# Gate and up projections wholly in 64-row tiles, q, k and v projections as single pieces, in a scheduled attention-and-MLP kernel

## The chip, the core and the metric

The kernel runs on one core of one Trainium2 chip. The metric is the device time of one execution in microseconds (us). The kernel before took 230.38 us (median of 3 runs, 229.4 to 230.75).

## What is computed

The input is x, 2048 rows of 448 in bf16. With xn = layernorm(x), two blocks work on xn, and the output is x + A(xn) * silu(B(xn)).

```
q, k, v = xn @ wq, xn @ wk, xn @ wv          # 448 -> 16 heads of 28, four segments of 512 rows
per segment: p = softmax(q k^T * scale + causal mask);  a_dot = p v
             a_mem = (phi(q) M) / (phi(q) z + 1e-6)   # memory of the segments before
             o = g * a_mem + (1 - g) * a_dot;  M += phi(k)^T v;  z += sum phi(k)
A(xn) = o @ wo
B(xn) = (gelu(xn @ w_gate) * (xn @ w_up)) @ w_down    # 448 -> 1792 -> 448
```

## The kernel before, in words

**Stages.** The four segments of 512 rows go through stages in the order G0, A0, A1, G1, A2, G2, A3, G3, D3 (table `ORDER`). G is the gate and up projection of a segment with its gelu. A is the attention of a segment. Into the A stages the kernel fits the down projection of the segment before (`down`, L1155), the output projection (`finish`, L1185), the memory's read and update (L898, L860) and the q, k and v projections of segments to come (`Unit.product`, L714). D3 is the down and output projection of the last segment.

**The order of work.** Every piece of work is an `Op` with a name, its engines with assumed durations, what it depends on, and the buffers it takes. `arrange` (L276) lists all ops in one order: at each step it takes the piece that can start first, or, among those within 0.2 us, the one with the lowest priority. The priorities come from the table `PRIO` (about 1000 numbers), and `STEP` says behind which of the ten score steps of an attention stage a filler piece is let go. The result is a fixed instruction order on each engine, which every engine then works through from front to back, waiting on semaphores. The planner also knows the array's mode (`Op.mode`): "full" for 128 contraction rows, "r64" for two tiles of 64 rows side by side, "r32" for four of 32 rows (the scores, where a head has 28 channels), "c32" for four column tiles (p times v).

**Buffers.** PSUM's eight banks are one pool `B_`: four in two pairs (`pp`), four single (`ps`). A chunk of gate and up takes two banks, a score step two pairs, any other product one bank. SBUF has, among others, five slots `pt` for the softmax numerators of a score step.

**Contraction over 448.** 448 is three times 128 and a rest of 64. In `gate_up` each of the 14 chunks of 128 hidden columns needs gate and up, each over 448 rows. `full` (L1089) makes the six matmuls over 128 rows (three for gate, then three for up, 512 columns each). The rests of gate and up lie in the two halves of one weight tile `wh_sb`, so `halves` (L1104) makes both rests at once, as two 64-row tiles side by side. To change modes seldom, the rests of four chunks are made in one visit: the visit ends two chunks and begins the next two (`VISITS`), four visits per segment. `hidden` then runs gelu on ScalarE (L1114) and the product of gelu and up on VectorE (L1119) into hT.

**Projections.** A q, k or v unit is one block of 128 rows by 448 columns: three matmuls over 128 rows (`Unit.full`), and a rest over 64 rows. Two units with even and odd block make their rests in one `visit` side by side (L714 again). In `project` the two full parts and the visit are three pieces, which the planner may set apart.

**Attention.** A score step has four matmuls side by side into two bank pairs, one or two times (L985), then two exponentials of 1024 columns on ScalarE (L1000), then causal masks on POOL (L1011). p times v is L1047, its copy out of PSUM L883. The exponentials need another table in ScalarE than gelu, so each passage between G and A stages has an ACT_TABLE_LOAD.

**Start.** Segment 0 is turned by TensorE (`turned_by_pe`, L596): once centred for the projections, once normalised (xn) for gate and up, four blocks each. The copies out of PSUM are L598, on VectorE or ScalarE. Meanwhile ScalarE also evicts projections (L752), squares weights for a bound that is checked once (L1248), and makes the first phi(k) (L826). The other segments' xn is turned by DMA (L685). Weights and x come by DMAs from the SP and ACT queues (L490).

## Time and profile before

| | |
|---|---|
| median of 3 runs | 230.38 us (229.4 to 230.75) |
| span of the profiled execution, first to last instruction | 227.6 us |
| TensorE (PE) busy | 217.5 us (96%), 1557 matmuls recorded |
| VectorE (DVE) busy | 152.7 us (67%) |
| ScalarE (ACT) busy | 152.7 us (67%) |
| GpSimd (POOL) busy | 129.3 us (57%) |
| granted TensorE clock | 0.999 |

The profile tells of one execution by its span, the time from its first to its last instruction. The times of runs are device times of whole executions, so they hold some 2.8 us outside the span (230.38 less 227.6). In rows of groups, the columns are line, engine and operation with "out<-in" by the program's names, shapes and count, then busy us and mean ns of one, then idle time of the engine just before them and what ended it. In rows of the timeline they are start, length, engine, line and operation, with idle time before and its releaser in brackets. A matmul's mean ns holds the way through the array, so start to start is the pace, not the mean. "PEld" is TensorE's weight load, which runs beside matmuls.

### The profile page before, as it was taken

How to read it: one execution, taken by the hardware profiler on the slowest of the kernel's cores; microseconds unless marked ns; L12 is line 12 of the kernel's file. 1: busy time of each engine (PE TensorE's matmuls, PEld its weight loads, DVE VectorE, ACT ScalarE, POOL GpSimd, SP SyncE). 2: the span in 40 equal slices, each digit the busy share in tenths (PEclk: the TensorE clock that was granted, in tenths of full speed). 3: DMA queues.
4: the chain of work that ended last, by engine and by line, in shares of the span. 5: the costliest groups of instructions: out<-in, count | busy, mean ns of one | idle time of the engine just before them, and what ended most of it. 6: DMA issues, size and time to landing. Idle time of an engine off the chain costs nothing.

```text
span 227.6 us, 4462 instructions
## 1 busy us (share of the span) xinstructions
PE 217.5 (96%) x1557; PEld 95.6 (42%) x1570; DVE 152.7 (67%) x287; ACT 152.7 (67%) x212; POOL 129.3 (57%) x221
## 2 busy tenths in 40 slices
PE   7999999889999999999999999999999999999991
PEld 2544433333544434344444444344444434444561
DVE  3799998767965795674875587863746463647262
ACT  4799645999898779432788898443878875346120
POOL 8601400579588599603599989853199477604500
PEclk9999999999999999999999999999999999999999
DMA  6999569964434763217603132272500018135011
GB/s 215 222 357 259 103 152 248 237 128 83 48 72 72 183 127 74 76 38 201 186 20 68 27 71 69 59 196 59 140 1 4 12 45 225 31 84 125 4 40 50
DMA packets 44708, 25.11 MB, mean 110 GB/s; under 512 B 30808, under 2 KB 40856, under 8 KB 44680
## 3 DMA queue, kind: packets, MB, share of 16 engines
q1 hardware_dynamic: 43704, 24.05, 44.7%
q10 hardware_dynamic: 976, 0.71, 1.0%
q8 instruction: 14, 0.23, 0.4%
q14 instruction: 14, 0.11, 0.2%
HBM read 16.00 MB, written 2.98 MB: 83 GB/s over the span
## 4 chain that ended last, share of the span: by engine, by line
PE 82%; ACT 10%; DVE 2%; issue 2%; ACTq 1%; POOL 1%; DVEq 0%; POOLq 0%
PE ps L1155 16%; PE ps L1089 15%; PE pp L1089 14%; PE ps L714 11%; PE pp L985 5%; PE ps L1185 5%; PE ps L1047 4%; ACT pt L1000 3%; PE ps L1104 3%; PE pp L1104 3%; PE pp L1155 2%; ACT pt L1248 2%; PE ps L898 1%; PE ps L860 1%; PE ps L1221 1%
## 5 line engine op out<-in xcount | busy, mean ns | idle before, releaser
L1000 ACT ACTIVATE pt<-pp 128x1024 bf16<-128x1024 f32 x75 | 73.3, 1037 | 11.8 <-PE pp L985 9.9
L1011 POOL TENSOR_SCALAR_AFFINE_SELECT pt<-pt 128x256 bf16<-128x256 bf16 x128 | 54.3, 448 | 26.0 <-ACT pt L1000 23.6
L1155 PE MATMUL ps<-wd_sb,hT 128*128 128x448 bf16 x182 | 39.0, 354 | 0.4 <-DVE qs L750 0.4
L1114 ACT ACTIVATE gl<-pp 128x512 bf16<-128x512 f32 x28 | 15.8, 595 | 29.0 <-PE pp L1104 23.2
L1155 PEld LDWEIGHTS <-hT 128*128 128x128 bf16 x210 | 18.8, 98 | 20.1 <-issue 5.0
L1119 DVE TENSOR_TENSOR hT<-gl,pp 128x512 bf16<-128x512 bf16 x28 | 18.4, 682 | 11.6 <-ACT gl L1114 11.5
L1119 DVE TENSOR_TENSOR hT<-gl,ps 128x512 bf16<-128x512 bf16 x28 | 18.7, 677 | 11.0 <-ACT gl L1114 8.4
L1114 ACT ACTIVATE gl<-ps 128x512 bf16<-128x512 f32 x28 | 16.6, 597 | 13.0 <-PE ps L1089 6.1
L1089 PEld LDWEIGHTS <-wu_sb 128*128 128x128 bf16 x168 | 16.4, 98 | 20.1 <-issue 0.3
L1089 PEld LDWEIGHTS <-wg_sb 128*128 128x128 bf16 x168 | 14.9, 98 | 22.5 <-issue 7.1
L909 POOL TENSOR_TENSOR om<-om,rb 128x512 f32<-128x512 f32 x12 | 14.9, 1268 | 15.9 <-DMA rb<-rdr 15.8
L714 PEld LDWEIGHTS <-xnT 128*128 128x128 bf16 (+1 forms) x192 | 15.0, 96 | 20.6 <-issue 10.1
L1089 PE MATMUL pp<-xnT,wu_sb 128*128 128x512 bf16 x84 | 22.7, 379 | 0.3
L1089 PE MATMUL ps<-xnT,wu_sb 128*128 128x512 bf16 x83 | 22.5, 379 | 0.2
L956 POOL TENSOR_TENSOR oT<-oa,om 128x512 bf16<-128x512 f32 x12 | 16.0, 1337 | 11.5 <-DVE oa L953 11.5
L1089 PE MATMUL ps<-xnT,wg_sb 128*128 128x512 bf16 x81 | 22.1, 380 | 0.3 <-issue 0.3
L1089 PE MATMUL pp<-xnT,wg_sb 128*128 128x512 bf16 x76 | 21.2, 380 | 0.4 <-issue 0.3
L831 POOL TENSOR_SCALAR e<-e 128x896 bf16<-128x896 bf16 (+1 forms) x12 | 12.8, 1070 | 10.9 <-ACT e L826 10.9
L985 PE MATMUL pp<-qT,kT 32*128 32x512 bf16 (+3 forms) x238 | 17.0, 301 | 2.0 <-ACT pt L1000 1.8
L646 POOL TENSOR_TENSOR rs<-rs,nhalf 128x1 f32<-128x1 f32 (+1 forms) x7 | 6.1, 882 | 16.1 <-DVE rs L641 16.1
L883 DVE COPY oa<-ps 128x512 f32<-128x512 f32 x16 | 10.9, 683 | 5.2 <-PE ps L1047 5.0
L1176 POOL TENSOR_TENSOR oo<-sg,x_sb 128x448 bf16<-128x448 f32 x12 | 12.4, 1037 | 2.7 <-DVE sg L1196 2.7
(121 smaller groups left out, 325.3 us busy)
## 6 DMA issues: line engine op xcount, KB each, us to landing
rb<-rdr SPq DMA_DIRECT2D x28, 256.0 KB
out_dram<-oo SPq DMA_DIRECT2D x15, 112.0 KB
wd_sb<-in_B_w_down_dram SPq DMA_DIRECT2D x2, 784.0 KB
x_sb<-in_A_x_dram SPq DMA_DIRECT2D x3, 448.0 KB
rdr<-dc SPq DMA_DIRECT2D x28, 32.0 KB
wg_sb<-in_B_w_gate_dram SPq DMA_DIRECT2D x2, 384.0 KB
wu_sb<-in_B_w_up_dram SPq DMA_DIRECT2D x2, 384.0 KB
wg_sb<-in_B_w_gate_dram SPq DMA_DIRECT2D x1, 576.0 KB
```

Source lines behind the costliest of these rows:

```text
L714: nc.tensor.matmul(out=self.bank.ap()[:, 0:D], lhsT=self.xT.ap()[r, c, n * P:(n + 1) * P], rhs=self.w[r, c, :], **kw)
L831: o = gps(f"mi{nm}{s}{half}", n / 1024, lambda: nc.gpsimd.tensor_scalar(out=t(), in0=t(), scalar1=1.0, scalar2=0.0, op0=ALU.min, op1=ALU.max),
L909: oU[s, g, 1] = t, gps(f"sm{s}{g}", 1.22, lambda t=t, r=r: nc.gpsimd.tensor_tensor(out=t.ap(), in0=t.ap(), in1=r.ap(), op=ALU.mult), deps= ...
L956: oT[s][1].append(gps(f"cb{s}{g}", 1.22, lambda g=g, t=t, tm=tm: nc.gpsimd.tensor_tensor(out=dst.ap()[:, g, :], in0=t.ap(), in1=tm.ap(), o ...
L985: nc.tensor.matmul(out=S2[i // 2].ap(i % 2)[:, c0:c0 + n], lhsT=kT[s][0].ap()[r, g, kb * P:(kb + 1) * P], rhs=qT[s][0].ap()[r, g, kb * P:L ...
L1000: nc.scalar.activation(out=dst, in_=src, func=ACT.Exp, scale=scale)
L1011: nc.gpsimd.affine_select(out=v, in_=v, pattern=[[0, 2], [1, P]], compare_op=ALU.is_ge, fill=0.0, base=0, channel_multiplier=-1)
L1089: nc.tensor.matmul(out=bf[fc].ap(i), lhsT=w[:, c, fc * P:(fc + 1) * P], rhs=xT.ap()[:, c, :], start=begins and c == 0, stop=not begins and ...
L1104: nc.tensor.matmul(out=bf[fc].ap(i), lhsT=wh_sb[r, fc * P:(fc + 1) * P], rhs=xT.ap()[r, NC3, :], start=fc in begins, stop=fc in ends)
L1114: a = act(f"ge{s}{fc}", L, lambda: nc.scalar.activation(out=gl.ap(), in_=bf[fc].ap(0), func=ACT.Gelu_apprx_tanh), func="gelu", deps=[o], a ...
L1119: nc.vector.tensor_tensor(out=hT[s][0].ap()[:, fc, :], in0=gl.ap(), in1=bf[fc].ap(1), op=ALU.mult), deps=[a] + held,
L1155: nc.tensor.matmul(out=bank.ap()[:, 0:D], lhsT=hT[s][0].ap()[:, fc, b * P:(b + 1) * P], rhs=wd_sb[:, fc, :], start=(fc == 0), stop=(fc == ...
```

## The change

**Gate and up.** The two weights lie in one tile `wgu_sb` of seven 64-row chunks, gate on partitions 0 to 63, up on 64 to 127. A chunk of hidden columns is now seven pairs of 64-row matmuls, gate and up side by side, and no 128-row matmul. A pair needs the same 64 rows of xn on both halves of the partitions, so beside xnT there is a copy with halves swapped (`other`). `part(fc, 0)` makes four pairs from xnT, `part(fc, 1)` the other three from the copy, and the first part of the next chunk stands ahead of the second part of this one. For segment 0 TensorE makes the copy, with three more 128-column turns per block and one more copy out of PSUM of 384 columns (`eo`). For the others two DMAs of 192 KB swap the halves within SBUF, after the seventh score step of the same segment. The copy lies in one of the five `pt` slots.

**Projections.** Two units are one piece `pj`: six matmuls over 128 rows and the pair of rests. `tail_first` puts the rests first where the array is not in "full" mode, and last where it is.

**Order.** `PRIO`, `STEP` and the new `BANKS` (which bank pairs a chunk may take) hold new numbers, so all engines' orders change. phi pieces of all segments are now let go by `STEP`.

```diff
-        if e == "PE" and o.mode and o.mode != mode:
+        if e == "PE" and o.flex:
+            o.tail_first = mode != "full"
+            s, mode = s + SWITCH * (mode not in ("full", "r64")), "full" if o.tail_first else "r64"
+        elif e == "PE" and o.mode and o.mode != mode:
             s, mode = s + SWITCH, o.mode
...
-        wg_sb = const.tile([P, NC3, F], BF16, name="wg_sb")
-        wu_sb = const.tile([P, NC3, F], BF16, name="wu_sb")
-        wh_sb = const.tile([P, F], BF16, name="wh_sb")
+        wgu_sb = const.tile([P, D // HALF, F], BF16, name="wgu_sb")
...
-            gu_in += [[load("SP", f"{n}{lo}", dst[:, :, r], ap[0:NC3 * P, r].rearrange(
-                "(c p) n -> p c n", p=P), 96 * (hi - lo)) for n, dst, ap in (
-                    ("wg", wg_sb, B_w_gate), ("wu", wu_sb, B_w_up))]] * (hi - lo)
+            gu_in += [[load("SP", f"{n}{lo}", wgu_sb[rows, :, r], ap[:, r].rearrange("(k p) n -> p k n", p=HALF),
+                            112 * (hi - lo)) for n, rows, ap in (
+                                ("wg", slice(0, HALF), B_w_gate), ("wu", slice(HALF, P), B_w_up))]] * (hi - lo)
...
+            n = W4 if shifted is None else W4 + NC3 * P
...
+            if shifted is not None:
+                to, eos = shifted
+                eos.append(evict(f"eo0{b}", 215, True, lambda copy: copy(
+                    out=to.ap()[:, 0:NC3, b * P:(b + 1) * P],
+                    in_=tp.ap().bitcast(BF16)[:, W4:n].rearrange("p (c t) -> p c t", t=P)),
...
-                fs = [u.full() for u in us]
-                o = visit("wr{}{}{}".format(s, *pair[0]), us, -9500.0)
...
+                    first = o_of[us[0]].tail_first
+                    if first:
+                        tails(True)
+                    for u in us:
+                        for c in range(NC3):
+                            u.product(c, start=not first and c == 0, stop=first and c == NC3 - 1)
+                    if not first:
+                        tails(False)
...
-            bf = [Buf(B_, TWO if fc in (10, 11) else APART if fc > 11 else ANY) for fc in range(NFC)]
+            bf = [Buf(B_, (ANY, TWO, APART)[BANKS.get(f"gu{s}{fc}", 0)]) for fc in range(NFC)]
...
+                other, moved = Buf(pt_p), []
+                for i in range(2):
+                    moved.append(dma(f"xs{s}{i}", 192, lambda i=i: nc.sync.dma_start(
+                        out=other.ap()[side[i], 0:NC3, :], in_=xT.ap()[side[1 - i], 0:NC3, :]), deps=xd,
+                        after=moved + att[s][6:7], prio=at(ph, -20), acq=[] if i else [other],
+                        uses=[xT] + ([other] if i else [])))
...
+            def part(fc, turn):
...
                 def mm():
-                    for fc in ends + begins:
+                    of = (other if turn else xT).ap()
+                    for c in range(NC3 + 1 - turn):
                         for i in range(2):
-                            r = slice(i * HALF, (i + 1) * HALF)
-                            nc.tensor.matmul(out=bf[fc].ap(i), lhsT=wh_sb[r, fc * P:(fc + 1) * P],
-                                             rhs=xT.ap()[r, NC3, :], start=fc in begins, stop=fc in ends)
+                            nc.tensor.matmul(out=bf[fc].ap(i), lhsT=wgu_sb[side[i], chunk(c, i, turn), fc * P:(fc + 1) * P],
+                                             rhs=of[side[i], c, :], start=not turn and c == 0,
+                                             stop=turn == 1 and c == NC3 - 1)
...
-            for ends, begins in VISITS:
-                for fc in ends:
-                    full(fc, True)
-                h = halves(ends, begins)
-                for fc in ends:
-                    hidden(fc, h)
-                for fc in begins:
-                    a = hidden(fc, full(fc, False))
+            part(0, 0)
+            for fc in range(NFC):
+                if fc < NFC - 1:
+                    part(fc + 1, 0)
+                h = part(fc, 1)
+                a = hidden(fc, h)
...
 PRIO = {
-    "ag00": -1122.63, "ag01": -1135.403, "ag10": -834.064, "ag11": -1044.988, "ag12": -837.494,
...
+    "exwq21": 429, "exwq30": 580, "exwq31": 560, "ez0": 302, "ez1": 300, "fa00": 439, "fa01": 709,
```

**What stands where.** The next rows are TensorE's in stage G0, where before the fourth begun chunk ends and the first long visit starts (L1089 the 128-row matmuls, L1104 the rests; `wu_sb` up, `ps` single banks).

```order
L1089 LDWEIGHTS wu_sb
L1089 MATMUL ps_93<-xnT_98,wu_sb 128x512
L1104 LDWEIGHTS wh_sb
L1104 MATMUL ps_94<-xnT_98,wh_sb 128x512
L1104 LDWEIGHTS wh_sb
L1104 MATMUL ps_95<-xnT_98,wh_sb 128x512
```

With the change the same stage reads so, at the seam of a second part (from the copy, `pt`) and the first part of the next chunk but one (from xnT); all are L1143.

```order
L1143 LDWEIGHTS wgu_sb
L1143 MATMUL pp_89<-pt_106,wgu_sb 128x512
L1143 LDWEIGHTS wgu_sb
L1143 MATMUL ps_90<-xnT_96,wgu_sb 128x512
L1143 LDWEIGHTS wgu_sb
L1143 MATMUL ps_91<-xnT_96,wgu_sb 128x512
```

Before, the array's mode changes there and changes back eight matmuls on; after, both sides of the seam are 64-row tiles, and stage G0 has no change of mode.

ScalarE's rows at the start, before (with buffer numbers), from its eviction of the first k block up to the first gelu; L752 evicts projections, L1248 squares weights, L826 is the exponential of phi(k).

```order
L752 ACTIVATE kn0_86<-ps1_93,rs0_144 128x16x28
L752 ACTIVATE kn0_86<-ps0_92,rs0_144 128x16x28
L1248 ACTIVATE pt0_108<-wq_sb_70 64x448
L1248 ACTIVATE pt1_109<-wk_sb_72 128x448 x3
L1248 ACTIVATE pt1_109<-wk_sb_72 64x448
L826 ACTIVATE e0_105<-kn0_86 128x32x28
L752 ACTIVATE hT_85<-ps3_95,rs0_144 128x16x28
L752 ACTIVATE hT_85<-ps1_93,rs0_144 128x16x28
L1114 ACT_TABLE_LOAD
L1114 ACTIVATE gl0_127<-pp0_90 128x512
```

After, the same stretch (L769 evicts projections, L606 copies the swapped xn, L865 is phi(k), L1290 squares).

```order
L769 ACTIVATE kn0_84<-pp0_88,rs0_142 128x16x28
L606 COPY pt0_106<-pp1_89 128x3x128
L865 ACTIVATE e0_103<-kn0_84 128x32x28
L1290 ACTIVATE pt1_107<-wq_sb_70 128x448
L606 COPY pt0_106<-pp0_88 128x3x128
L1290 ACTIVATE pt1_107<-wq_sb_70 64x448
L1290 ACTIVATE pt2_108<-wk_sb_72 128x448
L769 ACTIVATE hT_83<-ps3_93,rs0_142 128x16x28
L769 ACTIVATE hT_83<-ps2_92,rs0_142 128x16x28
L865 ACTIVATE e1_104<-kn0_84 128x32x28
L1155 ACT_TABLE_LOAD
L1155 ACTIVATE gl0_125<-pp1_89 128x512
```

Two copies of the swapped xn and the second exponential of phi(k) have come in ahead of the first gelu, and three of the four squares of wk have moved behind it.

ScalarE's rows where A1 passes into G1, before: the last score step's exponentials (L1000), an exponential of phi(q), gelu.

```order
L1000 ACTIVATE pt4_112<-pp0_90 128x1024
L1000 ACTIVATE pt4_112<-pp1_91 128x1024
L826 ACTIVATE e1_106<-qT0_100 128x1024
L1114 ACT_TABLE_LOAD
L1114 ACTIVATE gl1_128<-ps1_93 128x512
L1114 ACTIVATE gl0_127<-pp0_90 128x512
```

And after, from the last exponentials (L1039) on.

```order
L1039 ACTIVATE pt3_109<-pp0_88 128x1024
L1155 ACT_TABLE_LOAD
L1155 ACTIVATE gl2_127<-ps0_90 128x512
L1155 ACTIVATE gl0_125<-ps1_91 128x512
L865 ACT_TABLE_LOAD
L865 ACTIVATE e1_104<-qT0_98 128x1024
L1155 ACT_TABLE_LOAD
L1155 ACTIVATE gl1_126<-pp1_89 128x512
```

The exponential of phi(q) has moved behind the first two gelus, with a change of table on either side of it.

108 lines of the change are left out of this document (62 added, 46 removed), and 367 rows, old and new, of tables (BANKS, PRIO, STEP).

## The prediction

> **What bounds the kernel now.** First the profile's page: span, busy shares, the granted clock and the chain that ended last.
>
> ```profile
> span 227.6 us, 4462 instructions
> PE 217.5 (96%) x1557; PEld 95.6 (42%) x1570; DVE 152.7 (67%) x287; ACT 152.7 (67%) x212; POOL 129.3 (57%) x221
> PEclk9999999999999999999999999999999999999999
> PE 82%; ACT 10%; DVE 2%; issue 2%; ACTq 1%; POOL 1%; DVEq 0%; POOLq 0%
> ```
>
> TensorE bounds the kernel: busy 96% of the span, 82% of the chain, at full clock throughout. ScalarE, with 10% of the chain, comes next. So the question is what TensorE's time is made of, and where ScalarE holds it up. For the first I read TensorE's timeline in stage G0 around one visit to the rests (L1104), the thing that the change abolishes.
>
> ```profile
> 33.60 0.81 PE L1089 MATMUL pp<-xnT,wg_sb 128*128 128x512 bf16 x3
> 34.25 0.81 PE L1089 MATMUL pp<-xnT,wu_sb 128*128 128x512 bf16 x3
> 34.99 0.61 PE L1104 MATMUL pp<-xnT,wh_sb 64*128 64x512 bf16 x4
> 35.43 0.59 PE L1104 MATMUL ps<-xnT,wh_sb 64*128 64x512 bf16 x4
> 35.96 0.82 PE L1089 MATMUL ps<-xnT,wg_sb 128*128 128x512 bf16 x3
> ```
>
> Start to start, three 128-row matmuls take 0.65 us, so one takes 0.217. From 34.99 to 35.43 stand four 64-row matmuls, two pairs, in 0.44: a pair takes 0.22, as long as one 128-row matmul. Going in costs 34.99 - 34.25 - 0.65 = 0.09, coming out 35.96 - 35.43 - 0.44 = 0.09; with rounding I call a change of mode 0.10. There is no idle time beside it. For the second question I read TensorE and ScalarE at the start of A0.
>
> ```profile
> 38.66 0.39 PE L985 MATMUL pp<-qT,kT 32*128 32x512 bf16 x4
> 43.56 0.39 PE L985 MATMUL pp<-qT,kT 32*128 32x256 bf16 x6 [1.01 <-ACT pt L1000]
> 46.20 1.10 PE L1155 MATMUL ps<-wd_sb,hT 128*128 128x448 bf16 x5 [0.35 <-DVE qs L750]
> 49.19 0.39 PE L985 MATMUL pp<-qT,kT 32*128 32x512 bf16 x2 [0.48 <-ACT pt L1000]
> 38.11 0.60 ACT L1114 ACTIVATE gl<-ps 128x512 bf16<-128x512 f32 x1 [0.70 <-PE ps L1089]
> 38.73 1.28 ACT L1000 ACT_TABLE_LOAD   x1
> 40.02 1.94 ACT L1000 ACTIVATE pt<-pp 128x1024 bf16<-128x1024 f32 x2
> ```
>
> Two exponentials take 1.94 us and a score step gives two, so ten steps need 19.4 us of ScalarE. The first can start only after the last gelu and the table, 40.02 - 38.66 = 1.36 us after the first scores. TensorE then waits three times, 1.84 us together. Later stages are balanced more closely; the windows of A0, A1, A2 and A3:
>
> ```profile
> 38.70:62.00 23.30, 21.45 (x204) 9.30 (x203) 18.32 (x40) 22.00 (x28) 15.63 (x32) 1.00 0.73 133
> 62.00:88.70 26.70, 26.70 (x245) 11.70 (x245) 19.93 (x35) 22.87 (x29) 22.40 (x41) 1.00 0.50 103
> 111.60:139.00 27.40, 27.40 (x238) 12.44 (x236) 19.26 (x30) 23.47 (x27) 23.82 (x40) 1.00 0.23 53
> 162.00:186.00 24.00, 23.45 (x201) 10.13 (x200) 15.14 (x26) 20.06 (x23) 17.22 (x33) 1.00 0.06 14
> ```
>
> In the order PE, PEld, DVE, ACT, POOL, clock, share of DMA, GB/s: in A0 ScalarE is at 22.0 of 23.3 us, in A1 and A2 TensorE never idles.
>
> **The change part by part.** *Matmuls.* A chunk had six 128-row matmuls and one pair; now it has seven pairs: 7 x 0.216 = 1.51 us both times. The projections keep theirs. So the array's own time stays, and what moves is changes of mode. Counted along the two programs' orders there are 158 before and 123 after: in and out of gate and up 41 before, some 14 after (only p times v, one output projection, the scores and the down projection still border on it), of the projections 51 before, 46 after. That is 35 x 0.10 = **-3.5 us**, on the engine that sets the end.
>
> *Turns at the start.* Four blocks get three more 128-column turns.
>
> ```profile
> 14.18 0.39 PE L596 MATMUL pp<-oT,xn 128*128 128x128 bf16 x4
> 14.41 1.78 PE L714 MATMUL ps<-wq_sb,xnT 128*128 128x448 bf16 x10
> 16.03 0.59 PE L1104 MATMUL pp<-xnT,wh_sb 64*128 64x512 bf16 x4
> ```
>
> Four turns take 14.41 - 14.18 = 0.23 us, twelve more 0.69: **+0.7**, in front of G0, nothing hides it.
>
> *Copies at the start.* Four copies of 384 columns come in, two on VectorE, two on ScalarE. The 512-column copies bound them from above, and nothing from below:
>
> ```profile
> L598 DVE COPY xnT<-ps 128x512 bf16<-128x512 bf16 x4 | 1.7, 422 | 1.1 <-PE ps L596 1.1
> L598 ACT COPY xnT<-ps 128x512 bf16<-128x512 bf16 x2 | 1.0, 573 | 0.0
> 18.30 1.28 ACT L1114 ACT_TABLE_LOAD   x1
> 22.00 0.95 ACT L826 ACTIVATE e<-kn 128x896 bf16<-128x896 bf16 x1
> 14.44 1.97 ACT L1248 ACTIVATE pt<-wk_sb 128x448 bf16<-128x448 bf16 x4
> ```
>
> Ahead of the first table load ScalarE gets two such copies (at most 1.1, I take 0.95), one more 512-column copy (0.57) and the second exponential (0.95), and loses three squares (1.97 for four, so 1.5): about 1.0 later, so table at 19.3, first gelu at 20.6. Gelu and product (0.60 and 0.68, rows below) free the first chunk's banks at about 22.0. The fifth chunk needs them four first parts and three second parts after G0 starts (16.7): 4 x 0.86 + 3 x 0.65 = 5.4, at 22.1. It just fits. The fourth chunk's gelu stands behind two more table loads (1.28 each) with the gate's exponentials, as before, and may hold the eighth by 0.3. I take **+0.2**, bounds 0 and 1.0.
>
> *Later first exponentials.* This is the price of the new form. Before, gate's matmuls stood ahead of up's, so the last gelu ran while up was still made. Now the pairs end both together, so the last gelu starts when the stage is over: 0.2 for the array, 0.60 gelu, 1.28 table, 2.1 us after the first scores instead of 1.36. What it does to TensorE depends on the filler behind the first score step. The rows of A2 and A3:
>
> ```profile
> 111.24 0.39 PE L985 MATMUL pp<-qT,kT 32*128 32x512 bf16 x4
> 115.27 0.40 PE L985 MATMUL pp<-qT,kT 32*128 32x384 bf16 x8
> 113.01 1.94 ACT L1000 ACTIVATE pt<-pp 128x1024 bf16<-128x1024 f32 x2
> 161.62 0.39 PE L985 MATMUL pp<-qT,kT 32*128 32x512 bf16 x4
> 165.48 0.40 PE L985 MATMUL pp<-qT,kT 32*128 32x384 bf16 x8
> 162.99 1.94 ACT L1000 ACTIVATE pt<-pp 128x1024 bf16<-128x1024 f32 x2
> ```
>
> Before, 4.0 us (A2) and 3.9 us (A3) of filler cover first step and exponentials (done 3.7 and 3.3 after the scores): no wait. After, the order has two q pieces there in A2: 12 matmuls at 0.19 (0.217 x 448/512), two pairs at 0.19, the scores, four changes, 3.3 us; in A3 3.5. The second step needs both bank pairs, free at 2.1 + 1.9 = 4.0. So TensorE waits 0.7 and 0.5; a lower bound is 0, if the gelu is done earlier. I take **+0.6** and **+0.4**. In A0, ScalarE sets the pace; its first exponential comes at G0's end + 2.1. G0 ends 0.9 (its changes) and 0.3 (a small matmul moved to A0) earlier and 0.9 later, so it starts 0.4 later than before: I take **+0.2** for A0 and A1, bounds -0.8 (TensorE waits at A0's start that go) and +1.0.
>
> *Waits that may go.* A3's end has one that the fillers moved from A2 can cover:
>
> ```profile
> 185.93 0.39 PE L985 MATMUL pp<-qT,kT 32*128 32x384 bf16 x6 [0.30 <-ACT pt L1000]
> ```
>
> With the 0.26 us ahead of A3's sixth step it makes 0.56; I take **-0.4**.
>
> *At nothing.* The weights come as 896 KB before the first chunk, where 1216 KB came. The first gate weights were issued at 8.4 and G0 starts at 16.0; the rows below give the issue and the GB/s of the 40 slices of 5.7 us, of which the first three hold these loads. At half the least of them, 108 GB/s, 896 KB take 8 us, so even that is about covered; at the rate shown they take 4.
>
> ```profile
> 8.37 0.59 SPq L490 DMA_DIRECT2D wg_sb<-in_B_w_gate_dram  x1
> GB/s 215 222 357 259 103 152 248 237 128 83 48 72 72 183 127 74 76 38 201 186 20 68 27 71 69 59 196 59 140 1 4 12 45 225 31 84 125 4 40 50
> ```
>
> The swaps are two DMAs of 192 KB per segment, issued after the seventh score step; three steps of some 2.7 us (27.4 for ten in A2) and two first parts (1.7) follow, 9 us, and at the 103 GB/s of A1's window 384 KB take 3.7. With the cover gone they would cost up to 3.7 each. Six issues at 0.59 pass on SP, in front of dens and rb of the combination, which the chain does not hold. The lost `pt` slot binds only if a step must wait for p times v of four steps before, which stands ahead of it in the order: 0 to 0.4 per stage. The 1.28 us table loads in G1 delay the third gelu by 3.6, but the seventh chunk, which needs its banks, stands 10 us into the stage, the gelu's end at about 9.7: 0 to 0.3.
>
> *Sum.* -3.5 + 0.7 + 0.2 + 0.6 + 0.4 + 0.2 - 0.4 = -1.8. The profiled execution goes from 227.6 to 225.8, and the median, 2.8 us more for what lies outside the span, from 230.4 to **228.6 us**.
>
> **The rivals.** *ScalarE eats it (no change).* Of the 35 changes 27 are in G stages. If every A stage is ScalarE's pace from its first exponential on, each passes on the whole 0.7 us: -3.5 + 0.7 + 0.2 + 4 x 0.7 = +0.2, 230.6 us. For it: A0, 94% ScalarE. Against it: A1 to A3 have ScalarE idle 4 us each.
>
> *Bank rotation (slower).* Each chunk now must be evicted in turn, where four were begun and ended together.
>
> ```profile
> L1114 ACT ACTIVATE gl<-ps 128x512 bf16<-128x512 f32 x28 | 16.6, 597 | 13.0 <-PE ps L1089 6.1 <-PE ps L1104 5.8 <-PE pp L1104 0.5
> L1119 DVE TENSOR_TENSOR hT<-gl,ps 128x512 bf16<-128x512 bf16 x28 | 18.7, 677 | 11.0 <-ACT gl L1114 8.4 <-PE ps L1089 2.4
> ```
>
> From a chunk's last pair 0.2 + 0.60 + 0.68 and two handovers make about 1.6 us, against 1.51 per chunk. With four bank pairs in turn there are 3.0 us, enough; with three, every chunk waits 0.1 and whatever else VectorE has in the way, 56 x 0.1 = 5.6: 228.6 + 5.6 = 234.2 us. It decides where p times v and the output projection hold single banks in a G stage. The order has four pairs in turn in most places.
>
> *Weight loads stand in line (slower).* Were the load of a 64-row tile to wait for the matmul running in the same rows, each pair would take 0.22 and a load of 0.094.
>
> ```profile
> L1104 PEld LDWEIGHTS <-wh_sb 64*128 64x128 bf16 x112 | 4.4, 94 | 9.0 <-issue 5.8
> ```
>
> 56 chunks x 7 x 0.094 = 36.8 us more, 265 us. The rows of the visit above speak against it: two pairs after each other, in the same rows, at 0.22. [...]
>
> *The change does not do what it says.* The mode changes go but were hidden in waits: then only +0.7 and the later exponentials are left, 231 to 232 us. Against it: the visit's rows show no wait beside them.
>
> **How the numbers follow.** A measurement of this kernel can tell about 0.5%, 1.15 us. Forecast, with gains from 1.2 to 5: 0.62. ScalarE eats it: 0.20. Bank rotation: 0.10. Change hidden: 0.05. Weight loads: 0.02; the last 0.01 is another gain. Faster 0.63, same 0.20, slower 0.17. The range reaches down to all of -2.8 with 1.8 of A0's waits gone (-4.6, 225.8), and up over the no-change case and the nearer part of the slower ones, to 231.6.
>
> **What would show it.** Changes at 0.10 and pairs at 0.216 all through G0; stages G1, G2, G3 some 0.7 shorter except G1; first exponentials 2.1 us after the first scores; waits of TensorE at the second score step of A2 and A3. Wrong would be idle time of TensorE inside G stages released by VectorE (rotation), or a pair pace above 0.22.

## The result, and the profile after

The changed kernel took **239.27 us** (median, 237.89 to 241.01) against 229.89 us (229.38 to 230.75) for the kernel before, run beside it: 1.040 times the time, 95% interval 1.034 to 1.047. It is 9.4 us slower, where 1.8 us faster was forecast. The profiled execution has a span of 239.3 us, and is the longest of its runs, so stage times below add up to 11.7 us of loss and not 9.4.

The page of after: span, busy shares, granted clock, and the chain that ended last by engine and by line.

```profile
span 239.3 us, 5177 instructions
PE 218.5 (91%) x1918; PEld 100.0 (42%) x1918; DVE 157.6 (66%) x288; ACT 158.8 (66%) x218; POOL 127.2 (53%) x221
PEclk9999999999999999999999999999999999999998
PE 59%; DMA 21%; DVE 8%; SPq 6%; issue 2%; ACT 1%; POOL 1%; DVEq 0%; ACTq 0%
```

TensorE's busy time is nearly what it was (218.5 after 217.5), its clock too (0.996 after 0.999), but its share of the chain fell from 82% to 59%. DMA, which the chain before did not show at all, now has 21% and SP's queue 6%. TensorE waits, and what ends the waits is a transfer. Where, tell the stages, each from its first matmul to the next stage's first:

| stage | before | after | difference |
|---|---|---|---|
| start | 16.03 | 17.30 | +1.3 |
| G0 | 22.63 | 27.83 | **+5.2** |
| A0 and A1 | 49.82 | 52.57 | +2.8 |
| G1 | 22.76 | 24.51 | +1.8 |
| A2 | 27.61 | 26.48 | -1.1 |
| G2 | 22.77 | 22.02 | -0.8 |
| A3 | 24.63 | 27.49 | +2.9 |
| G3 and D3 | 41.35 | 41.09 | -0.3 |

Nearly half of the loss is in G0. The windows of G0 in the kernel before, and of G0 and G2 in the kernel after (columns as in the prediction):

```profile
16.03:38.66 22.63, 22.30 (x114) 8.91 (x115) 21.45 (x51) 15.01 (x24) 3.66 (x3) 1.00 0.89 197
```

```profile
17.30:45.13 27.83, 22.31 (x199) 10.49 (x196) 20.48 (x48) 15.57 (x26) 2.83 (x3) 1.00 1.00 183
148.70:170.70 22.00, 22.00 (x218) 9.72 (x212) 12.96 (x18) 10.92 (x16) 9.68 (x12) 1.00 0.28 74
```

G2 is what the change was worth on the array: no idle time, 22.0 us. In G0 TensorE is busy for the same 22.3 us as before and stands idle for 5.5. Five of the rows of TensorE's waits, summed over the whole span and with the longest (columns: us in total, times, longest):

```profile
PE ps L731 <- DVE hT L1160: 3.2, 2, 2.1
PE ps L1143 <- DVE hT L1160: 2.6, 2, 2.3
PE pp L1143 <- DVE hT L1160: 1.8, 2, 1.3
PE pp L1024 <- ACT pt L1039: 1.2, 2, 0.9
PE ps L1143 <- DMA pt<-xnT: 1.2, 1, 1.2
```

Gate and up (L1143) wait for VectorE's product of gelu and up (L1160), that is, for a bank. This looks like the rival of bank rotation. But rows from the timeline of TensorE in G0 show that the waits come seldom and most are long:

```profile
24.13 1.04 PE L1143 MATMUL pp<-xnT,wgu_sb 64*128 64x512 bf16 x8 [1.27 <-DVE hT L1160]
25.64 1.04 PE L1143 MATMUL pp<-xnT,wgu_sb 64*128 64x512 bf16 x8
26.50 0.83 PE L1143 MATMUL pp<-pt,wgu_sb 64*128 64x512 bf16 x6
27.15 1.04 PE L1143 MATMUL ps<-xnT,wgu_sb 64*128 64x512 bf16 x8
29.93 0.37 PE L1143 MATMUL ps<-xnT,wgu_sb 64*128 64x512 bf16 x1 [1.08 <-ACT gl L1155]
37.64 1.02 PE L1143 MATMUL ps<-xnT,wgu_sb 64*128 64x512 bf16 x7 [2.29 <-DVE hT L1160]
```

From 25.64 to 27.15 a whole chunk, four pairs and three, takes 1.51 us without a wait; if rotation by itself were the limit, a wait would stand at every chunk. So I ask what VectorE and ScalarE did before such a wait. VectorE and then ScalarE:

```profile
20.21 1.68 DVE L640 BATCH_NORM_STATS2 st<-x_sb 128x6 f32<-128x448 bf16 x3 [1.63 <-DMA x_sb<-in_A_x_dram]
35.90 1.09 DVE L883 SCALAR_TENSOR_TENSOR kn<-kn,e 128x896 bf16<-128x896 bf16 x1 [3.07 <-DMA kT<-kn]
36.91 0.68 DVE L1160 TENSOR_TENSOR hT<-gl,ps 128x512 bf16<-128x512 bf16 x1
```

```profile
23.51 1.28 ACT L583 ACT_TABLE_LOAD   x1
27.67 0.20 ACT L583 ACTIVATE igate<-betac 128x1 f32<-128x1 bf16 x1 [2.88 <-DMA betac<-in_A_beta_dram]
27.98 1.28 ACT L1155 ACT_TABLE_LOAD   x1
29.28 0.60 ACT L1155 ACTIVATE gl<-ps 128x512 bf16<-128x512 f32 x1
```

Both engines work their list from front to back. VectorE first waits 1.63 us for x of segment 1, and the statistics of that segment stand ahead of the product for which TensorE waits 1.27. Later it waits 3.07 us for the transposes of k (it may overwrite kn only when they are done), and again the product that TensorE needs stands behind: the waits of 2.29 and, just after it, 0.53 end with it. ScalarE waits 2.88 us for beta, and a table load and the fourth gelu stand behind: TensorE waits 1.08 and then 0.35. These five waits are the 5.5 us of idle time in G0. In the kernel before ScalarE came to beta at 22.85 and found it there:

```profile
22.85 0.19 ACT L578 ACTIVATE igate<-betac 128x1 f32<-128x1 bf16 x1
```

Beta and the transposes are on SP's queue behind the weights. SP's timeline, after and before:

```profile
13.61 1.86 SPq L497 DMA_DIRECT2D betac<-in_A_beta_dram  x1
15.60 10.42 SPq L780 DMA_TRANSPOSE kT<-kn  x3
26.11 5.14 SPq L780 DMA_TRANSPOSE qT<-hT  x4
31.31 1.26 SPq L780 DMA_TRANSPOSE kT<-kn  x1
```

```profile
14.86 6.88 SPq L763 DMA_TRANSPOSE kT<-kn  x4
```

Beta is issued 0.5 us later than before (13.61 after 13.12) and the first transpose 0.7 later, but three transposes now hold SP for 10.42 us where four held it for 6.88, and the fourth stands behind those of q. The weights ahead of them are slow. The window from 11.4 to 17.1 us, after and before (last two columns: share of DMA busy, GB/s):

```profile
11.40:17.10 5.70, 5.55 (x45) 2.90 (x44) 5.29 (x14) 5.51 (x12) 0.93 (x1) 1.00 1.15 205
```

```profile
11.40:17.10 5.70, 5.54 (x43) 2.69 (x42) 5.33 (x13) 5.70 (x12) 0.00 (x0) 1.00 1.08 358
```

The DMA engines are busy in both, and move 205 GB/s instead of 358. In the mean over the trace's packets, one of 1536 bytes takes 129 ns after and 69 before, one of 1024 bytes 87 and 54; the last weights come at 26.8 us instead of 21.1. What has changed in them is the shape: gate goes to partitions 0 to 63 alone and up to 64 to 127, where six sevenths went to all 128. The planner prices these loads at 320 GB/s (`rate=320.0` in `load`), so its order puts what stands behind them where it would be in time at that rate.

The rest of the loss is spread. In A0 and A1 TensorE has 47.9 us of work, as before (48.0), and idles 4.7 us instead of 1.8: it waits 1.1, 1.1 and 0.9 us for work of VectorE that comes late, and 1.2 us for exponentials. In G1 TensorE waits for the swapped copy, in A3 for a bank again, behind a wait of VectorE for `rb` (L992):

```profile
101.07 0.80 PE L1143 MATMUL ps<-pt,wgu_sb 64*128 64x512 bf16 x5 [1.16 <-DMA pt<-xnT]
173.47 1.59 PE L731 MATMUL ps<-wv_sb,xnT 64*128 64x448 bf16 x7 [2.07 <-DVE hT L1160]
```

```profile
172.13 0.69 DVE L992 TENSOR_TENSOR oa<-oa,rb 128x512 f32<-128x512 f32 x1 [2.14 <-DMA rb<-rdr]
```

SP's timeline tells why the swap of segment 1 is late: G1 starts at 97.70.

```profile
95.76 0.54 SPq L1126 DMA_DIRECT2D pt<-xnT  x1
97.04 0.59 SPq L1126 DMA_DIRECT2D pt<-xnT  x1
```

### The profile page after: what moved, and what is told of

Same layout as the page of the kernel before. It is cut to its first block, busy times and chain, and to the rows that moved or that the text cites. A ratio compares the mean times of both kernels' runs of the same rounds, so it can differ in the third digit from the quotient of the medians.

```text
span 239.3 us, 5177 instructions
## 1 busy us (share of the span) xinstructions
PE 218.5 (91%) x1918; PEld 100.0 (42%) x1918; DVE 157.6 (66%) x288; ACT 158.8 (66%) x218; POOL 127.2 (53%) x221
## 4 chain that ended last, share of the span: by engine, by line
PE 59%; DMA 21%; DVE 8%; SPq 6%; issue 2%; ACT 1%; POOL 1%; DVEq 0%; ACTq 0%
PE ps L1194 15%; PE ps L1143 11%; PE pp L1143 11%; PE ps L731 7%; DMA betac<-in_A_beta_dram 6%; PE pp L1024 4%; PE ps L1224 4%; PE ps L1086 3%; SPq L497 3%; DMA rb<-rdr 3%; DMA wk_sb<-in_A_wk_dram 2%; DVE hT L1160 2%; DMA kT<-kn 2%; DMA dc<-den 2%; SPq L780 2%
## 5 line engine op out<-in xcount | busy, mean ns | idle before, releaser
L1039 ACT ACTIVATE pt<-pp 128x1024 bf16<-128x1024 f32 x74 | 71.9, 1028 | 13.5 <-PE pp L1024 13.2
L1050 POOL TENSOR_SCALAR_AFFINE_SELECT pt<-pt 128x256 bf16<-128x256 bf16 x128 | 52.7, 438 | 28.7 <-ACT pt L1039 27.9
L1143 PEld LDWEIGHTS <-wgu_sb 64*128 64x128 bf16 x784 | 39.1, 94 | 53.0 <-issue 10.3
L1194 PE MATMUL ps<-wd_sb,hT 128*128 128x448 bf16 x196 | 42.3, 353 | 0.0
L1143 PE MATMUL ps<-xnT,wgu_sb 64*128 64x512 bf16 x232 | 30.4, 376 | 3.7 <-DVE hT L1160 2.6
L1143 PE MATMUL pp<-xnT,wgu_sb 64*128 64x512 bf16 x216 | 28.4, 376 | 1.8 <-DVE hT L1160 1.8
L1160 DVE TENSOR_TENSOR hT<-gl,ps 128x512 bf16<-128x512 bf16 x29 | 19.7, 682 | 13.4 <-ACT gl L1155 13.2
L1143 PE MATMUL ps<-pt,wgu_sb 64*128 64x512 bf16 x174 | 24.2, 376 | 1.2 <-DMA pt<-xnT 1.2
L731 PEld LDWEIGHTS <-xnT 128*128 128x128 bf16 (+1 forms) x192 | 14.9, 96 | 24.3 <-issue 14.0
L1160 DVE TENSOR_TENSOR hT<-gl,pp 128x512 bf16<-128x512 bf16 x27 | 18.1, 680 | 9.1 <-ACT gl L1155 9.1
L1143 PE MATMUL pp<-pt,wgu_sb 64*128 64x512 bf16 x162 | 22.5, 376 | 0.0
L870 POOL TENSOR_SCALAR e<-e 128x896 bf16<-128x896 bf16 (+1 forms) x12 | 11.8, 986 | 11.8 <-ACT e L865 11.7
L731 PE MATMUL ps<-wv_sb,xnT 128*128 128x448 bf16 (+1 forms) x60 | 12.6, 354 | 2.6 <-DVE hT L1160 2.1
```

What stands on the lines that cost most here:

```text
L731: nc.tensor.matmul(out=self.bank.ap()[:, 0:D], lhsT=self.xT.ap()[r, c, n * P:(n + 1) * P], rhs=self.w[r, c, :], **kw)
L870: o = gps(f"mi{nm}{s}{half}", n / 1024, lambda: nc.gpsimd.tensor_scalar(out=t(), in0=t(), scalar1=1.0, scalar2=0.0, op0=ALU.min, op1=ALU.max),
L1039: nc.scalar.activation(out=dst, in_=src, func=ACT.Exp, scale=scale)
L1050: nc.gpsimd.affine_select(out=v, in_=v, pattern=[[0, 2], [1, P]], compare_op=ALU.is_ge, fill=0.0, base=0, channel_multiplier=-1)
L1143: nc.tensor.matmul(out=bf[fc].ap(i), lhsT=wgu_sb[side[i], chunk(c, i, turn), fc * P:(fc + 1) * P], rhs=of[side[i], c, :], start=not turn a ...
L1160: nc.vector.tensor_tensor(out=hT[s][0].ap()[:, fc, :], in0=gl.ap(), in1=bf[fc].ap(1), op=ALU.mult), deps=[a] + held,
```

## The experiments

Theory: loads onto half the partitions run at a lower rate, and beta, x of the next segments and the transposes, which stand behind them in the DMA queues, make ScalarE and VectorE late. Rivals: only the order of the queue is wrong, and moving one item mends it; or the new form itself, with its banks turned chunk by chunk, is slower whatever the loads do.

**dma_rates.** Nothing but loads of the first four chunks' weights (896 KB): `wide` as before, `halves` as after, `queues` with the two halves on two queues.

```diff
+        if n[:4] == "wide":
+            for i, w in enumerate((B_w_gate, B_w_up)):
+                nc.sync.dma_start(out=x[:, 3 * i + 1:3 * i + 4, 0:N], in_=w[0:384, r].rearrange("(c p) n -> p c n", p=P))
...
+        else:
+            nc.sync.dma_start(out=x[lo, :, 0:N], in_=gate(r))
+            (nc.sync if n[:4] == "halv" else nc.scalar).dma_start(out=x[hi, :, 0:N], in_=up(r))
```

> The kernel does none of the computation: it only loads the same 896 KB of gate and up weights (1 KB rows) six times, one stage after the other: 'wide' to all 128 partitions (two loads of 384 KB, two of 64 KB), 'halves' as the changed kernel does it (gate to partitions 0 to 63, then up to 64 to 127, both on SyncE's queue), 'queues' the same two loads but up on ScalarE's queue, so that both are under way together. Theory H (a load that goes to half of the partitions runs at about half the rate): packets of 1024 bytes take some 50 ns in wide and some 90 ns in halves, wide moves some 300 GB/s or more, halves some 200; queues, if the partitions written at one time are what counts, is back near wide. Rival R (the weights' form does not matter, the rates in the two profiles differ by what else was moving): all three at one rate, within 10%.

VectorE's copies, each waiting for the loads whose name stands to the right of the arrow:

```profile
10.15 0.18 DVE L27 COPY halves<-wide 128x7 bf16<-128x7 bf16 x1 [5.34 <-DMA wide<-in_B_w_up_dram]
17.30 0.18 DVE L27 COPY queues<-halves 128x7 bf16<-128x7 bf16 x1 [6.97 <-DMA halves<-in_B_w_up_dram]
24.74 0.18 DVE L27 COPY wide<-queues 128x7 bf16<-128x7 bf16 x1 [7.25 <-DMA queues<-in_B_w_up_dram]
```

5.3 against 7.0 us, with nothing else on the chip; a second pass gave 5.06, 6.95 and 7.04. A packet took 53 ns in the mean in the first wide load, 77 in halves, 75 with two queues. Two queues do not help here.

**up_act.** Up's loads on ScalarE's queue.

```diff
-            o = op(name, {eng: (0.5, 2.0)}, lambda: (nc.sync if eng == "SP" else nc.scalar).dma_start(
+            o = op(name, {eng: (0.5, 2.0)}, lambda: (nc.sync if eng == "SP" and name[:2] != "wu" else nc.scalar).dma_start(
```

> The changed kernel with one edit: the three loads of up's weights are issued by ScalarE and not by SyncE, so that gate's half of the partitions and up's are written at the same time. Theory H (the half-partition loads run at half rate; the beta table and the transposes of kn queue behind them, ScalarE and VectorE stand in line for those in stage G0, the banks are not freed, TensorE idles): loads over by about 21 us rather than 27, the wait of 2.88 us for the beta table gone, TensorE idle in G0 down from 5.5 us to 2 or less, time 232 to 235 us. Rival R (bank rotation: chunks are evicted one by one, with other work of VectorE and ScalarE in the way, whatever the loads do): idle in G0 stays at 4 us or more, time 238 to 240 us.

236.90 us, ratio 1.030 (1.027 to 1.033); G0 24.66 us. The wait for beta is gone, that for the transposes stays:

```profile
33.07 1.09 DVE L883 SCALAR_TENSOR_TENSOR kn<-kn,e 128x896 bf16<-128x896 bf16 x1 [2.46 <-DMA kT<-kn]
```

This lies between the theories: TensorE still idles 2.7 us in G0, where 2 or less was expected with the loads as the cause, and 4 or more with the rotation. The 1536-byte packets of both halves took only 76 ns here, against what dma_rates says of two queues; the 1024-byte ones stayed slow, 80 ns. What is left of the wait is in part a matter of order: the fourth transpose of k is issued at 28.64, behind the four of q, while the kernel before had all four of k ahead.

**beta_early.** Beta's load is issued ahead of the gate weights, nothing else moved.

```diff
+        beta_now, weights_now = beta_in.fn, gu_in[0][0].fn
+        beta_in.fn = lambda: None
...
+            beta_now()
+            weights_now()
```

> The changed kernel with one edit: the 0.2 KB load of the beta table is issued ahead of the gate and up weights, not behind them; every engine's order is otherwise the same. Theory H: ScalarE's wait of 2.88 us for it in G0 goes and with it TensorE's first stalls there (1.27, 1.08 and 0.35 us); VectorE's wait for the transposes of kn stays, so of the 2.7 us one to 2.7 are gained: 236.5 to 238.5 us. Rival R (rotation): the banks are late anyway, within 0.5 us of 239.3.

240.97 us, ratio 1.042 (1.036 to 1.047): a miss. ScalarE no longer waits for beta, but x of segment 1, which VectorE reads, now comes later, and the first wait of TensorE grows from 1.27 to 2.29 us. The expectation had put that wait of 1.27 down to beta; it was x's from the start.

```profile
21.09 1.68 DVE L647 BATCH_NORM_STATS2 st<-x_sb 128x6 f32<-128x448 bf16 x3 [2.65 <-DMA x_sb<-in_A_x_dram]
```

In all, TensorE's idle time in G0 falls from 5.5 to 4.4 us, and yet the kernel is no faster. The profile also has two stretches at half clock (25.3 to 28.7 and 49.2 to 56.0 us), which the kernels so far had not; how much of the time is theirs was not told apart.

**before_half.** The kernel before, with each of its six wide weight loads made as two of 64 partitions. Same bytes, same matmuls.

```diff
-            gu_in += [[load("SP", f"{n}{lo}", dst[:, :, r], ap[0:NC3 * P, r].rearrange(
-                "(c p) n -> p c n", p=P), 96 * (hi - lo)) for n, dst, ap in (
-                    ("wg", wg_sb, B_w_gate), ("wu", wu_sb, B_w_up))]] * (hi - lo)
+            gu_in += [[load("SP", f"{n}{lo}{h}", dst[h, :, r], ap[0:NC3 * P, r].rearrange(
+                "(c p) n -> p c n", p=P)[h], 48 * (hi - lo)) for n, dst, ap in (
+                    ("wg", wg_sb, B_w_gate), ("wu", wu_sb, B_w_up)) for h in (slice(0, HALF), slice(HALF, P))]] * (hi - lo)
```

> The kernel before with one edit: each of its six loads of gate and up weights onto 128 partitions is issued as two, to partitions 0 to 63 and then 64 to 127, same bytes and same 1 KB and 1.5 KB rows; that is six more issues on SyncE, some 0.6 us each, and nothing else. Theory H: packets of 1024 bytes go from some 50 to some 90 ns, the beta table and the transposes of kn come 4 us or more later, and the kernel before gets idle time of TensorE in G0 as well: 232 to 236 us. Rival R: the rate is the same, at most the 3.6 us of issues on SyncE are felt: 230 to 231.5 us.

232.86 us, ratio 1.015 (1.010 to 1.021), G0 25.06 us instead of 22.63. Waits of the same kind appear in the old kernel (beta as below, x of segment 1 by 1.3 us, though none for the transposes of k), and a 1024-byte packet takes 84 ns in the mean, a 1536-byte one 119:

```profile
ACT igate L578 <- DMA betac<-in_A_beta_dram: 2.8, 1, 2.8
PE ps L1089 <- DVE hT L754: 1.2, 1, 1.2
PE ps L1089 <- ACT gl L1114: 1.1, 1, 1.1
```

So the loads' shape alone makes G0 2.4 us longer, without any of the new matmuls. The six more issues on SP come with it, and beta is issued at 16.87 instead of 13.12. But the DMA engines are busy without a break from 11 to 23 us and move 217 to 263 GB/s, where the kernel before moved 333 to 364 in stretches of 3 us from 11 to 20; so it is their rate that is short, not SP.

**after_lean** and **before_lean.** Four of the six gate and up loads (chunks 4 to 13, 2240 of 3136 KB) are left out, and all chunks use the first four's weights.

```diff
-                            nc.tensor.matmul(out=bf[fc].ap(i), lhsT=wgu_sb[side[i], chunk(c, i, turn), fc * P:(fc + 1) * P],
+                            nc.tensor.matmul(out=bf[fc].ap(i), lhsT=wgu_sb[side[i], chunk(c, i, turn), fc % 4 * P:(fc % 4 + 1) * P],
...
+        for o in order:
+            if o.name in ("wg4", "wu4", "wg8", "wu8"):
+                o.fn = None
```

> The changed kernel without four of its six loads of gate and up weights (2240 of 3136 KB): all chunks use the weights of the first four, so the output is not the reference's; every engine's order stays. Theory H (what stands in the DMA queues behind the slow weight loads comes late, and the in-order engines wait for it): TensorE's idle time in G0 falls from 5.5 us to 1.5 or less, and the kernel is some 6 us faster, 232 to 234.5 us; what is left against the kernel before in the same form is the start, A0, A1 and G1, 2 to 4 us. Rival R (rotation of the banks by itself): idle in G0 stays at 4 us or more, 237 us or more.

> The kernel before without the same four loads (all chunks use the weights of the first four; not the reference's output), as the counterpart: it has no idle time in G0 to lose, so both theories expect 229 to 230.5 us. The difference between the two without these loads is what the new form costs or brings apart from them: theory H 2 to 4 us slower, rival R 7 us or more.

after_lean took 232.25 us, ratio 1.010 (1.006 to 1.013); before_lean 230.63, ratio 1.000 (0.996 to 1.005). G0 of after_lean, and below it of before_lean:

```profile
17.15:39.02 21.87, 21.69 (x199) 10.24 (x196) 20.42 (x49) 15.59 (x26) 2.97 (x3) 1.00 0.81 139
```

```profile
16.03:38.65 22.62, 22.30 (x113) 8.91 (x112) 20.96 (x50) 15.00 (x24) 3.66 (x3) 1.00 0.66 125
```

With the loads out of the way G0 falls from 27.83 to 21.87 us and is 0.75 shorter than before_lean's 22.62. Without them the changed kernel gains 7.0 us and the old one nothing: **7.0 of the 9.4 us are the loads**, and 6.0 of the 7.0 lie in G0. The new form by itself is 232.25 - 230.63 = 1.6 us slower, which is clear of the noise, if not by much. (7.0 and 1.6 are not quite 9.4, because the kernel before took 230.43 on the chip of these runs and 229.89 on that of the first.) Stage by stage after_lean against before_lean: start +1.1, G0 -0.75, A0 and A1 +1.85, G1 +1.6, A2 -1.3, G2 -0.75, A3 +1.0, G3 and D3 -1.1, together the 1.6 us of the spans (230.5 and 228.9).

**mended.** Up's loads on ScalarE's queue, beta early, and the fourth transpose of k ahead of those of q (beta_early's and up_act's edits, and this).

```diff
...
+        by = {o.name: o for o in order}
+        names = ("tq00", "tq02", "tq03", "tq01", "tk02")
+        fns = [by[n].fn for n in names]
+        for n, fn in zip(names, fns[-1:] + fns[:-1]):
+            by[n].fn = fn
...
```

> The changed kernel with three edits of when transfers are issued, and no other: up's weights by ScalarE, the beta table ahead of the gate weights, and the fourth transpose of kn on SyncE's queue ahead of the four transposes of q instead of behind them. Theory H: VectorE's wait of 2.5 to 3.1 us for the transposes of kn in G0 goes as well, and of TensorE's idle time there 1.5 us or less is left: 233.5 to 235.5 us. Rival R: as with up's loads on ScalarE alone, 236.5 to 237.5 us, since VectorE then has the next thing in the way.

238.03 us, ratio 1.035 (1.027 to 1.044): a miss. The wait for the transposes is gone, and two for x of segments 1 and 2 have taken its place; up_act alone waited 0.9 us for x of segment 1, so beta ahead of the weights adds to it. up_act with the fourth transpose alone moved was not run. This profile too has a stretch at half clock, from 45.5 to 48.9 us.

```profile
21.60 1.68 DVE L640 BATCH_NORM_STATS2 st<-x_sb 128x6 f32<-128x448 bf16 x3 [2.64 <-DMA x_sb<-in_A_x_dram]
38.54 1.15 DVE L640 BATCH_NORM_STATS2 st<-x_sb 128x6 f32<-128x448 bf16 x2 [2.33 <-DMA x_sb<-in_A_x_dram]
```

**late_wg8.** The last two weight loads (672 KB each) issued behind beta and the transposes of k. Each name on the left now issues what stands on the right (`wg`, `wu` the weights from that chunk on, `tq` and `tk` transposes).

```diff
+    "wg8": ["beta"], "wu8": [], "beta": [], "tq00": ["tk02", "wg8", "wu8"],
+    "tq02": ["tq00"], "tq03": ["tq02"], "tq01": ["tq03"], "tk02": ["tq01"]
```

> The changed kernel, whole, with the same loads in another order on SyncE's queue: the last two weight loads (672 KB each, for the chunks 8 to 13) are issued behind the beta table and the four transposes of kn, no longer ahead of them. The half rate stays, the bytes stay. Theory H (what cost G0 its time is what stood behind the slow loads): no wait of ScalarE for the beta table, none of VectorE for the transposes of kn, TensorE idle in G0 down from 5.5 us to 1.5 or less, 232.5 to 235 us. Rival (the slow loads cost G0 by themselves, through bytes that contend or weights that are late): idle of 3 us or more stays in G0, 236 us or more.

237.02 us, ratio 1.025 (1.015 to 1.035), G0 25.21 us. The waits for beta and the transposes are gone, but the time and the 3.2 us of idle time left in G0 are what the rival forecast. Now it is the weights that come late (below), and x by 1.87 and 2.48 us. The four transposes of k, issued with fewer weights ahead of them, hold SP for 6.80 us, as in the kernel before.

```profile
31.28 1.03 PE L1143 MATMUL pp<-xnT,wgu_sb 64*128 64x512 bf16 x7 [0.63 <-DMA wgu_sb<-in_B_w_up_dram]
```

**late_all.** late_wg8, with x of segment 1 ahead of the second pair of weights, the swap of segment 1 two places earlier on SP, and in A0 four pieces of VectorE that free banks ahead of others (`xs` swap, `hm` product of gelu and up, `evwk` evictions of k).

```diff
+    "wg4": ["x1"], "wu4": ["wg4"], "x1": ["wu4"],
+    "den110": ["xs10"], "tq22": ["xs11"], "xs10": ["den110"], "rd111": ["tq22"], "xs11": ["rd111"],
+    "xn20": [], "xn22": ["hm012"], "xn21": ["xn20"], "hm012": ["hm013"], "hm013": ["xn22", "xn21"],
+    "bn30": ["evwk11"], "xn23": ["evwk10"], "du20": ["xn23"], "bn32": ["du20"], "evwk11": ["bn30"], "evwk10": ["bn32"]
```

> The kernel of the run before it with three more moves: x of segment 1 is loaded ahead of the second pair of weight loads; the two swaps of segment 1 are issued two places earlier on SyncE's queue; and on VectorE, at the start of A0, the last two products of G0 and the two evictions of k come ahead of the normalising and the statistics of segments 2 and 3. Expected if the waits that are left (1.3 us in G1 for the swap; 1.1 and 1.1 us in A0 for a bank that VectorE frees late) are what the traces call them: 2.5 to 3.5 us less than that run, 229.5 to 232 us, that is within 1% of the kernel before. If instead the next thing in VectorE's or SyncE's order takes the place of each, 0 to 1.5 us less.

237.50 us, ratio 1.030 (1.024 to 1.036): no better. The weights are late by 1.2 us, x of segment 2 by 2.95; A0's waits for banks are gone, but those for the exponentials grow from 1.2 to 2.2 (3.4 us of this A0 ran at half clock):

```profile
PE pp L1024 <- ACT pt L1039: 2.2, 4, 1.1
PE pp L1143 <- DMA wgu_sb<-in_B_w_up_dram: 1.2, 1, 1.2
```

Every order makes something else late: beta and the transposes of k in the change as it is, x in beta_early and mended, weights and x in late_wg8 and late_all. up_act and late_wg8 give back 2.4 and 2.3 us, and no order gives back more. That speaks for DMA time itself being short in this stretch, and against the rival of a wrong order as far as these orders go; an order that gives back the rest is not ruled out.

**lean_all.** after_lean with late_all's last three lines (swap, VectorE in A0).

> The changed kernel without four of its six gate and up loads (as in the run after_lean, 232.25 us; all chunks use the weights of the first four), with two moves: the two swaps of segment 1 two places earlier on SyncE's queue, and at the start of A0 the last two products of G0 and the two evictions of k ahead of the normalising and the statistics on VectorE. It sizes the two terms of the sum that lie apart from the loads. If the swap's wait in G1 (1.3 us) and the two bank waits of A0 (1.1 and 1.1 us) are each lost time: 229 to 230 us. If A0 is paced by ScalarE from its first exponential on, so that the bank waits only fill time that it would lose anyway, and the swap alone counts: 230.5 to 231.5 us. If neither counts: 232 us or more.

234.45 us, ratio 1.011 (1.007 to 1.016), beside after_lean's 1.010; the kernel before spread from 229.5 to 233.95 on that chip, so that a gain of up to 1 us could hide. No gain is seen, which is the third of the expected outcomes. The waits for the swap and the banks are gone, and the scores wait for the exponentials instead. G1 without the swap's wait takes 24.26 us, where after_lean's took 24.35:

```profile
PE pp L1024 <- ACT pt L1039: 1.6, 4, 0.6
PE ps L731 <- DMA wv_sb<-in_A_wv_dram: 1.7, 1, 1.7
```

The second row is a wait at the start of the execution, of 0.4 us in after's profile. This one also has 3.4 us at half clock in A0, so its A0 is not compared.

**dma_rates2.** Again only loads: `four`, each half in two parts; `low`, both weights to partitions 0 to 63; `quarters`, four loads of 32 partitions; `three`, the wide six sevenths (768 KB) in halves.

> None of the computation, only weight loads in six stages, all on SyncE's queue, 1 KB rows: 'wide' (896 KB onto 128 partitions) and 'halves' (gate to 0 to 63, then up to 64 to 127) as measured before (5.3 and 6.9 us), 'four' (halves, each in two loads, taken in turn), 'low' (both to partitions 0 to 63), 'quarters' (four loads of 32 partitions each) and 'three' (768 KB as four loads of 64 partitions by 3 rows each). Theory H (the number of partitions that one load writes sets its rate): low and four as halves, 6.5 to 7.2 us, three about 6.0, quarters 9 us or more. Rival: the rate goes by the rows per partition (7 against 3): three as fast as wide for its bytes (4.7 us), quarters as halves.

Waits: wide 5.28, halves 6.87, four 6.49, quarters 6.37, three 5.82. `low` can't be read: one of its two loads was issued at the very start, ahead of `wide`. Loads to 32 partitions at a time are no slower than to 64, which I had expected at 9 us or more. More rows per load is not the cause: `three` has the old layout of rows, and its packets take 64 ns in the mean, where the wide ones of dma_rates took 53.

**dma_rates3.** 1344 KB in rows of 1.5 KB, as the later weights; `stagger`, each half in two loads of unequal size on two queues; `xlow`, 784 KB of x, contiguous in memory, onto halves.

> None of the computation, only loads, one stage after the other: 1344 KB of gate and up weights in rows of 1.5 KB, 'wide' (128 partitions), 'halves' (gate to 0 to 63, then up to 64 to 127, SyncE's queue), 'queues' (up on ScalarE's queue), 'stagger' (on two queues, each cut in two, so that the queues do not run in step), and 'xlow' (784 KB of x in rows of 896 bytes, contiguous in DRAM, to 0 to 63 and then 64 to 127). In the kernels rows of 1.5 KB took 70 ns onto 128 partitions, 119 to 138 ns onto 64, and 74 to 78 ns with up on ScalarE's queue. If two queues restore the rate for such rows, queues is as fast as wide (within 10%) and halves some 1.6 times as slow; if, as with rows of 1 KB, two queues do not help, queues is as halves. xlow: if the side of the destination sets the rate, rows of 896 bytes take 65 ns or more (41 to 55 ns in loads onto 128 partitions), if it is the weights' place in DRAM, 41 to 55 ns.

```profile
11.57 0.18 DVE L27 COPY halves<-wide 128x7 bf16<-128x7 bf16 x1 [6.76 <-DMA wide<-in_B_w_up_dram]
20.85 0.18 DVE L27 COPY queues<-halves 128x7 bf16<-128x7 bf16 x1 [9.10 <-DMA halves<-in_B_w_up_dram]
```

`queues` waits 9.01, `stagger` 8.40. Against dma_rates, 448 KB more cost 1.42 us wide and 2.13 us in halves, 323 and 215 GB/s. x to halves has slow packets as well (62 ns in the mean for 896 bytes, against 41.5 for x to 128 partitions in before_lean), though it is read from another place in another pattern. That speaks for the side written as what sets the rate.

## Why the prediction was wrong

**The step that failed is "At nothing"**, and in it the weights' loads. It divided 896 KB by half the least rate of the kernel before, 108 GB/s, and asked whether the first weights reach the first chunk. They did: G0 began at 17.30 without waiting for them. It did not ask what stands behind the 3136 KB in the same queues, nor at what rate that many bytes go onto half the partitions. In their place the runs show +7.0 us: with four of the six loads left out the changed kernel gains 7.0 and the old one nothing, and G0 falls from 27.83 to 21.87; and the old kernel with the same shape of loads waits for beta and x as well and loses 1.5%. The rest of the miss is in the new form: without these loads it is 1.6 us slower, where 1.8 faster was forecast. Two terms of the sum failed there, A0 and A1 (+1.85 for +0.2) and G1, which "At nothing" has without a price beyond its swaps and table loads (+1.6). The row to read stood in the prediction: the third slice of the GB/s, 357, is where the window above has the DMA engines busy all the time, so nothing was left there for slower packets.

What the step missed is a rate, and the runs give it: 205 GB/s in the window after where 358 stood before, 215 in halves against 323 wide from dma_rates to dma_rates3, and 32 partitions no slower than 64 (6.37 us and 6.87 in dma_rates2). At 215 and 323 GB/s the 3136 KB of weights would take 14.9 us instead of 9.9, an estimate from these two figures: 5.0 us longer. The trace has the last weights 5.7 us later. Passed on whole, the 5.0 would have made the forecast of -1.8 a loss. Two queues at once are no remedy in dma_rates and dma_rates3 (7.25 us against 6.97 on one, 9.01 against 9.10). The 1.5-KB rows of up_act did better, with 327 GB/s from 18 to 21 us on two queues; its 1-KB rows stayed slow, at 80 ns a packet.

Point by point:

- *Pace of pairs, 1.51 us a chunk.* Right, by the rows of G0 above. The rival of weight loads in line is refuted with it.
- *Changes of mode, -3.5.* Right where it shows: the G stages with next to no wait are 0.75 (G0 of after_lean, G2) and 0.85 (G3) shorter; forecast was 0.7. For G0 alone it was 1.2 (0.9 by changes, 0.3 by a matmul that moved), so there it falls short, 0.2 of it by idle time.
- *Turns and copies, +0.7 and +0.2.* The start is 1.1 to 1.3 longer, where 0.7 was taken; the rest was not traced. The first gelu came at 21.26 instead of the forecast 20.6; in after_lean G0 has 0.2 us idle, so the copies cost about what was taken.
- *Later first exponentials.* Right in time (2.0 us after the scores, 2.1 forecast), mostly wrong in effect: TensorE lost some 0.2 us at A2's second step (0.62 us for its eight matmuls instead of 0.40), where 0.6 was taken, and at A3, where 0.4 was taken, no wait stands at the second step in after_lean. The second step of A2 comes 3.8 us after the first, not the 3.3 that I added up, because the 16 matmuls of the filler with their change of mode take 3.5. The rows of after:

```profile
122.21 0.39 PE L1024 MATMUL pp<-qT,kT 32*128 32x512 bf16 x4
122.54 3.51 PE L731 MATMUL ps<-wq_sb,xnT 64*128 64x448 bf16 x16
125.99 0.62 PE L1024 MATMUL pp<-qT,kT 32*128 32x384 bf16 x8
```

- *A0 and A1, +0.2.* Mis-sized: +1.85 in the lean pair. In after_lean the k projection waits 1.0 for the last product's bank, the norms' matmul (L1300) 0.9 and the memory's (L899) 0.7. When the first two were taken away (lean_all, late_all) the scores waited for the exponentials instead. That speaks for ScalarE's pace in A0, the rival at 0.20, but both profiles have 3.4 us of A0 at half clock, so it is not shown, nor how much of the 1.85 it would explain.
- *Swaps, nothing.* Wrong: the cover was taken from when they may be issued, 9 us before use. On SP they stood behind transposes and the combination's transfers, 1.9 us before G1, and TensorE waited 1.2 us. That the wait is lost time is not shown: without it G1 took 24.26 us in lean_all, 24.35 with it in after_lean. What G1's +1.6 is made of stays open.
- *A3's end, -0.4.* In the lean pair A3's idle time falls from 0.55 to 0.14 us, which is the gain forecast. A3 is 1.0 longer all the same, by work moved there from A2: its busy time is 25.4 for 24.05, A2's 26.2 for 27.7. The 2.07 us at A3's start in after's profile appeared in no other kernel's, so it is most likely of that execution, which was the longest of its runs.
- *Bank rotation, 0.10.* It named the waiting engine rightly and the reason wrongly. With the loads out of the way G0 has 0.2 us of idle time; in these runs rotation bound only where VectorE or ScalarE was held by something else.
- *2.8 us outside the span* was the median of all runs less the span of one; after's profiled execution took 241.01 us for a span of 239.3, so 1.7 lies outside.

A version that beats both kernels was not found. Loads to all 128 partitions with the weights' old layout and pairs of rows from it were not tried.

## What to carry to other kernels

When a change alters the partitions that a load reaches, price its bytes anew, and then go down every queue behind it: what binds may be a small table that an in-order engine reads, not the weights themselves. A wait that names VectorE or ScalarE is not yet a cause; look for the wait of that engine just before it. And when every order of a queue that you try makes another item late, look whether the DMA engines are busy all the time: then fewer or faster bytes are the next thing to try.
